# Windowed softmax mix and cosine feed-forward on one core: the prologue's loads, conversions and second softmax in another order

## The chip, the cores and the metric

One core of a Trainium2 chip runs the kernel. The metric is the device time of one execution in microseconds. Three runs of the kernel before gave 2207.27 to 2207.57 us, with a median of 2207.28 us.

The core has a matrix engine (TensorE: PE in the profile, and PEld for its weight loads), a vector engine (VectorE, DVE), an activation engine (ScalarE, ACT), a general engine (GpSimd, POOL) and a sync engine (SyncE, SP) that here issues every transfer. Each engine takes its instructions strictly in the order in which the program lists them, and an instruction waits on semaphores for what it needs from the others.

## The reference

```python
w = np.exp(weight_gen - np.max(weight_gen, axis=-1, keepdims=True))
w = w / (np.sum(w, axis=-1, keepdims=True) + 1e-09)            # 8 heads, 7 taps
x_unf = x_pad[:, idx, :].reshape(B, S, K, H, group)             # a causal window of 7 rows
x = np.einsum('bshk,bskhg->bshg', w, x_unf).reshape(B * S, D)   # 32768 x 192
h = x @ w_in                                                    # 192 x 2048
g = h * np.cos(h)
return (g @ w_out).astype(np.float32)                           # 2048 x 192
```

`x` and `weight_gen` are 32 bits wide; `w_in` and `w_out` arrive as 64-bit words, which the kernel converts itself.

## The kernel before

**Blocks.** Each of the 128 partitions owns 256 consecutive rows of x. A block `b` is four of them in every partition, so there are 64 blocks of 512 rows. For each block the rows are mixed with their taps (`attention`: seven products on line 316 and six adds on line 331, all on POOL), turned over by PE, cut into a high and a low half (`split`: `x_hi` on ACT, `x_b` and `x_lo`), multiplied with `w_in` (`ffn_in_first` and `ffn_in_second`), taken through the cosine by ACT and DVE, cut into halves again (`ghi` on ACT, `glo` on DVE) and multiplied with `w_out` (`ffn_out`). The mixed rows of a block are called `xa` in the trace.

**The loop.** The main loop runs over `i`; eight values of `i` (pairs of 128-column slices of the hidden layer) make a block. In iteration `i` PE does the first product of `i` and the second product of `j = i - 8`. The tile `h` for the hidden values has three buffers in PSUM, and a buffer comes free when DVE has written `glo` (L449). From block 3 on the rows are turned over one at a time, inside `ffn_out` (L379); blocks 1 and 2 are turned over whole, at `i = 5` and `i = 13` (`transpose_all`, L370), and ACT copies the result out of PSUM (L712) before the tile is used for `h`.

**What sets the order.** The program is written by hand and nothing reorders it: the last lines of the function chain every instruction to the one ahead of it on its engine. The mixing of later blocks is a generator `bg` that is advanced two or three steps in each iteration; `until_mixed(b)` forces the rest of a block's steps ahead of the place that needs it. Block 3 is needed at `i = 14`, and its first row is turned over there.

**Weights.** A piece of `w_in` or `w_out` is loaded as 64-bit words into a buffer `raw` and converted by `two_parts` in steps: a size by ACT (L138) into a tile handed out by `make_room`, three integer steps on DVE (L140, L144, L148), a cast to the high half on ACT (L151, for `w_out` also L153 to the tile `wo_b`), and the low half on POOL (L154). The `raw` buffers are shared with `ghi`: twelve of them, handed round in turn, so that a `ghi` waits for the last reader (L154 on POOL) of the piece that had its buffer. Three pieces are loaded and converted ahead of the loop (`w_b0`, `w_a0`, `w_a1`). The others stand in the table `late`: (iteration after which it is loaded, iteration in which it is converted, kind, piece). `w_in_a` fills `wa_hi` and `wa_lo`, `w_in_b` fills `wb_hi` and `wb_lo`, and `w_out_2(q)` fills `wo` and `wo_b` for a pair of slices. I call the eight pieces of `w_out` wo0 to wo7 below.

**Softmax.** `sm0` makes the taps of block 0, `sm1` those of blocks 1 and 2, `sm2` those of blocks 3 to 6. `early=True` means that the exponential is done by ACT; in that case the sum over the taps and its scaling are done by DVE (L265, L268), and otherwise by POOL (`add_taps`, L189 and L192).

**Ahead of the loop.** Three of the four rows of block 0 are mixed by DVE (`mix_first`, L611 and L623) with PE adding up the parts while it turns them over (L603); the fourth row is mixed by POOL. Then come the conversions of `w_b0` and `w_a0`, the casts of block 0 (`x_hi`, `x_b`, `x_lo`) and `sm1`, then the conversion of `w_a1`, the maximum of `sm2`, and the first steps of block 1's mixing.

**SyncE.** The queue of SP holds the transfers and, among them, a marker after each `ffn_in_first` (`traded`), which ties the following instructions to a buffer that changes hands. A transfer that has to wait holds up what stands behind it on that queue.

Of the kernel before, what the change touches and what calls it, by code (L numbers as in the profile page):

```python
# [50 lines left out]
def tile_softmax_conv_then_cos_ffn(  # L51
# [34 lines left out]
    gpool = ctx.enter_context(tc.tile_pool(name="gpool", bufs=12))  # L86
# [37 lines left out]
    def make_room():  # L124
        sizes = ps_m.tile([P, 2, CT], F32, name="acc")
        room[:] = [sizes[:, n, 0:CW].bitcast(I32) for n in range(2)]
# [104 lines left out]
    def softmax(r0, r1, eng, early=True, to=None):  # L231
        n = (r1 - r0) * H
        if r0 == 0:
            t = const.tile([P, n, K], F32, name="taps0")
        else:
            tile_ = work.tile([P, RW * H, K], F32, name="taps")
            t = tile_[:, 0:n, :]
# [26 lines left out]
        if early:  # L264
            nc.vector.tensor_reduce(out=den, in_=t, axis=AX.X, op=ALU.add)  # L265
        else:
            add_taps(t, den)
        (nc.vector if early else nc.gpsimd).tensor_scalar(  # L268
# [287 lines left out]
    def all_of(*steps):  # L556
# [7 lines left out]
        (-1, 2, w_in_a, (1280, 1792)), (-1, 2, w_out_2, (1,)), (-1, 3, w_out_2, (2,)),  # L564
        (-1, 3, w_in_a, (1792, 2048)), (0, 4, w_out_2, (3,)), (0, 4, w_out_2, (4,)),
        (1, 5, w_out_2, (5,)), (1, 6, w_out_2, (6,)), (2, 6, w_out_2, (7,)),
# [17 lines left out]
    load_rows(0)  # L584
    w_b0 = w_in_b(0)
    w_a0 = w_in_a(0, 256)
    sm1 = softmax(R, 3 * R, nc.gpsimd)
# [18 lines left out]
    def mix_first():  # L606
# [9 lines left out]
        for n, ks in enumerate(((K - 1,), (0, 1), (2, 3), (4, 5))):  # L616
# [7 lines left out]
            add_transposed(tr, pr, range(RV), n == 0)  # L624
        return tr

    all_of(sm0)
    all_of(attention(0, nc.gpsimd, RV, R, "pr"))
    tr0 = mix_first()
    add_transposed(tr0, mixed[0], range(RV, R), False)  # L630
    transposed.add(0)
    make_room()
    go_on(w_b0, 1)
    go_on(w_a0, 1)
    x_hi, x_lo, x_b = parts_of(0)
    nc.scalar.copy(out=x_hi, in_=tr0)
    go_on(w_b0, 3)
    all_of(w_b0)
    nc.scalar.copy(out=x_b, in_=x_hi.bitcast(F32))
    go_on(sm1, 2)  # L640
    go_on(w_a0, 3)
    all_of(w_a0)
    nc.vector.tensor_tensor(out=x_lo, in0=tr0, in1=x_hi.bitcast(F32), op=ALU.subtract)
    go_on(sm1, 3)
    all_of(sm1)
# [10 lines left out]
    sm = sm2  # L656
    FIRST = NPAIR + 1
    for i in range(N + LAG + 1):
# [6 lines left out]
        if converts_now:  # L665
            make_room()
# [40 lines left out]
        all_of(*converts.pop(i - 1, ()))  # L707
        now, later = list(splits), []
        splits.clear()
        if whole is not None:  # L710
            t = work.tile([P, 2, CT], F32, name="part", bufs=2)
            nc.scalar.copy(out=t, in_=whole)  # L712
            later.append(split(b + 1, t, slice(0, CT), nc.vector))
        if 0 <= i - 1 < N:
            dve_fraction(i - 1)
            act_cos(i - 1)
# [15 lines left out]
        if i >= NPAIR - 2:  # L732
            next(sm, None)
        for _ in range(3 if i < 12 or i < 64 and i % 4 == 0 else 2):
# [42 lines left out]
```

## Time and profile before

| what | value |
|---|---|
| median of three runs | 2207.28 us |
| the profiled execution, its own time | 2208.1 us |
| its span | 2206.2 us |
| PE busy | 2151.6 us, 98% |
| POOL busy | 2000.7 us, 91% |
| DVE busy | 1907.6 us, 86% |
| ACT busy | 1862.9 us, 84% |
| mean granted PE clock | 0.99 |

The profiled execution takes 2208.1 us, of which the span from its first to its last instruction is 2206.2 us; it lies 0.8 us above the median of the runs. Rows of the timeline give a start, a duration, the engine, the line, and in brackets how long the engine had been idle before and what released it. `x2` in a row stands for two instructions of the same kind.

### The profile page before, as it was taken

What the parts mean: (1) busy time and instruction counts of PE and PEld (TensorE: products, weight loads), DVE (VectorE), ACT (ScalarE), POOL (GpSimd) and SP (SyncE); (2) the same over time, 40 slices, a digit from 0 to 9 for tenths busy, and PEclk for the clock granted to TensorE, in tenths of its full rate; (3) what the DMA queues carried; (4) which work ended last, traced back from release to release, by engine and by line L of the source; (5) the groups of instructions that cost most, each with busy time, mean ns of one, the idle gap of its engine ahead of it and who ended that gap; (6) DMA issues with size and microseconds to landing.
All of it is one profiled execution on the core that took longest, in us unless ns stands there. A gap on an engine that the chain in (4) does not pass through costs nothing.

```text
span 2206.2 us, 62053 instructions
## 1 busy us (share of the span) xinstructions
PE 2151.6 (98%) x26516; PEld 1676.4 (76%) x26516; DVE 1907.6 (86%) x1671; ACT 1862.9 (84%) x2278; POOL 2000.7 (91%) x1687
## 2 busy tenths in 40 slices
PE   4699999999999999999999999999999999999998
PEld 2478777777777777777777777777877777777777
DVE  7888888888888888888888888888888888888886
ACT  4788888888888888888888888888888888888885
POOL 7999999999999999999999999999899999989830
PEclk8799999999999999999999999999999999999999
DMA  7121221221221221221221221211211212211100
GB/s 182 45 48 34 57 48 42 48 48 43 48 57 31 60 48 30 60 48 39 52 48 39 52 56 30 60 46 33 60 41 46 49 41 49 48 40 45 30 16 19
DMA packets 53282, 105.65 MB, mean 48 GB/s; under 512 B 5790, under 2 KB 42134, under 8 KB 53006
## 3 DMA queue, kind: packets, MB, share of 16 engines
q1 hardware_dynamic: 53006, 101.69, 19.3%
q8 instruction: 208, 3.41, 0.7%
q14 instruction: 68, 0.56, 0.1%
HBM read 76.50 MB, written 25.17 MB: 46 GB/s over the span
## 4 chain that ended last, share of the span: by engine, by line
PE 94%; POOL 4%; DVE 1%; issue 1%; DMA 0%; ACT 0%; SPq 0%; POOLq 0%; DVEq 0%; ACTq 0%
PE acc L491 47%; PE h L417 30%; PE h L400 15%; POOL xa L331 1%; PE acc L379 1%; POOL pr L316 1%; PE h L491 0%; POOL wo L154 0%; DMA xt<-in_x_dram 0%; POOL xa L316 0%; POOL wa_lo L154 0%; POOL taps L249 0%; DVE pr L611 0%; POOL taps L281 0%; DVE glo L449 0%
## 5 line engine op out<-in xcount | busy, mean ns | idle before, releaser
L431 DVE TENSOR_TENSOR turn<-h,turn 128x1024 f32<-128x1024 f32 x512 | 627.1, 1225 | 262.8 <-ACT turn L427 258.0
L491 PE MATMUL acc<-wo,ghi 64*128 64x384 f32 x8096 | 808.7, 337 | 0.3 <-ACT ghi L445 0.2
L491 PEld LDWEIGHTS acc<-wo,ghi 64*128 64x128 f32 x8096 | 724.9, 184 | 54.6 <-ACT part L513 16.4
L435 ACT ACTIVATE turn<-turn 128x1024 f32<-128x1024 f32 x512 | 542.4, 1059 | 199.4 <-DVE turn L431 199.3
L331 POOL TENSOR_TENSOR xa<-xa,pr 128x768 f32<-128x768 f32 (+1 forms) x384 | 698.6, 1819 | 0.8
L438 DVE SCALAR_TENSOR_TENSOR h<-h,turn 128x1024 f32<-128x1024 f32 x512 | 631.2, 1233 | 4.6 <-ACT turn L435 4.6
L449 DVE TENSOR_TENSOR glo<-h,ghi 128x1024 bf16<-128x1024 f32 x512 | 622.1, 1215 | 3.8 <-ACT ghi L445 3.8
L427 ACT ACTIVATE turn<-h 128x1024 int32<-128x1024 f32 x512 | 524.6, 1025 | 89.6 <-PE h L417 79.8
L316 POOL TENSOR_TENSOR pr<-xt,taps 128x768 f32<-128x768 f32 (+1 forms) x384 | 589.1, 1534 | 6.3
L445 ACT CAST ghi<-h 128x1024 fp32r<-128x1024 f32 x512 | 516.4, 1009 | 7.5 <-POOL wb_lo L154 5.7
L491 PE MATMUL acc<-wo_b,glo 64*128 64x192 bf16 x8096 | 462.4, 243 | 0.1
L491 PEld LDWEIGHTS <-glo 64*128 64x128 bf16 (+1 forms) x8128 | 317.6, 94 | 85.4 <-issue 67.4
L400 PE MATMUL h<-x_hi,wa_hi 64*128 64x512 f32 x1024 | 300.3, 581 | 0.0
L417 PE MATMUL h<-x_hi,wa_hi 64*128 64x512 f32 x1024 | 300.1, 581 | 0.0
L400 PE MATMUL h<-x_lo,wa_hi 64*128 64x512 bf16 x1024 | 199.2, 384 | 28.6 <-DVE glo L449 20.8
L417 PE MATMUL h<-x_hi,wb_hi 64*128 64x512 f32 x1024 | 204.6, 395 | 0.0
L400 PE MATMUL h<-x_b,wa_lo 64*128 64x512 bf16 x1024 | 196.6, 379 | 2.3 <-POOL wa_lo L154 2.3
L417 PE MATMUL h<-x_lo,wa_hi 64*128 64x512 bf16 x1024 | 195.7, 378 | 2.5 <-SPq L342 1.8
L417 PE MATMUL h<-x_b,wb_lo 64*128 64x512 bf16 x1024 | 195.9, 378 | 0.0
L417 PE MATMUL h<-x_lo,wb_hi 64*128 64x512 bf16 x1024 | 195.9, 378 | 0.0
L417 PE MATMUL h<-x_b,wa_lo 64*128 64x512 bf16 x1024 | 195.9, 378 | 0.0
L359 POOL TENSOR_SCALAR x_b<-x_hi 128x256 bf16<-128x256 f32 (+1 forms) x246 | 102.9, 418 | 93.0 <-ACT x_hi L357 91.7
(90 smaller groups left out, 1973.1 us busy)
## 6 DMA issues: line engine op xcount, KB each, us to landing
xt<-in_x_dram SPq DMA_DIRECT2D x62, 960.0 KB, 7.0
out_dram<-part SPq DMA_DIRECT2D x256, 96.0 KB, 2.2
taps<-in_weight_gen_dram SPq DMA_DIRECT2D x15, 448.0 KB, 4.4
raw<-in_moe_w_out_dram SPq DMA_DIRECT2D x8, 384.0 KB, 9.4
raw<-in_moe_w_in_dram SPq DMA_DIRECT2D x10, 256.0 KB, 11.5
xt<-in_x_dram SPq DMA_DIRECT2D x1, 768.0 KB, 11.5
xt<-in_x_dram SPq DMA_DIRECT2D x1, 540.0 KB, 5.5
raw<-in_moe_w_in_dram SPq DMA_DIRECT2D x4, 128.0 KB, 7.9
```

The lines of the kernel that those rows point to most:

```text
L316: eng.tensor_tensor(out=dst.rearrange("p r (h g) -> p r h g", h=H), in0=xt[:, k + ra:k + rb, :].rearrange("p r (h g) -> p r h g", h=H), in ...
L331: eng.tensor_tensor(out=acc if k < K else xa, in0=acc, in1=old[:, ra:rb], op=ALU.add)
L359: nc.gpsimd.tensor_scalar(out=near[:, :, cs], in0=hi[:, :, cs].bitcast(F32), scalar1=1.0, scalar2=1.0, op0=ALU.mult, op1=ALU.mult)
L400: nc.tensor.matmul(h[:, q, :], lhsT=w[rs, chunk(pair, q)], rhs=v[rs, q, :], start=(m == 0), stop=False, skip_group_check=True)
L417: nc.tensor.matmul(h[:, 1 - q, :], lhsT=w[rs, cs], rhs=v[rs, q ^ middle, :], start=False, stop=(m == len(prods) - 1), skip_group_check=True)
L427: nc.scalar.activation(out=t.bitcast(I32), in_=hs[i], func=AF.Identity, bias=0.25, scale=1.0)
L431: nc.vector.tensor_tensor(out=t, in0=hs[i], in1=t.bitcast(I32), op=ALU.subtract)
L435: nc.scalar.activation(out=t, in_=t, func=AF.Sin, bias=SIN_BIAS, scale=SIN_SCALE)
L438: nc.vector.scalar_tensor_tensor(out=hs[i], in0=hs[i], scalar=TWO_PI, in1=turns.pop(i), op0=ALU.mult, op1=ALU.mult)
L445: nc.scalar.copy(out=hi, in_=hs[i])
L449: nc.vector.tensor_tensor(out=lo, in0=hs.pop(i), in1=hi.bitcast(F32), op=ALU.subtract)
L491: nc.tensor.matmul(to, lhsT=g[rs, n, t * P:(t + 1) * P], rhs=w[rs, fc, :], start=(lo == 0 and c == 0 and (k == 0 or whole and k == 1)), st ...
```

## The change

Nothing that is computed changes. The order of the prologue does, in seven places:

1. The taps of block 0 are taken in rising order (0, then 1 and 2, 3 and 4, 5 and 6); before, tap 6 came first.
2. The two pieces `w_a0` and `w_b0` trade places, in their loads and their conversions.
3. `sm1` is moved forward: its maximum stands among the products of `mix_first`, and its steps among the conversions of `w_a0` and `w_b0`. Its sum over the taps is done by POOL (`on_dve=False`).
4. The buffers shared by `raw` and `ghi` become thirteen.
5. In the table `late`, four pieces are loaded after iteration 0 instead of ahead of the loop, and the pieces of `w_out` from wo3 on are converted one an iteration (wo3 at 4, wo4 at 5, up to wo7 at 8) where before wo3 and wo4 stood at 4 and wo6 and wo7 at 6. The size of the piece at iteration 8 goes to an SBUF tile (`part`), since by then the PSUM tile `acc` is in use.
6. In the iteration in which a block is turned over whole, ACT's copy of it (`part<-h`) stands ahead of the casts of the weights converted then; before it stood behind them.
7. The generator `bg` is advanced by two steps instead of three for `i` below 8; `sm2` takes its last steps one iteration later.

```diff
-    gpool = ctx.enter_context(tc.tile_pool(name="gpool", bufs=12))
+    gpool = ctx.enter_context(tc.tile_pool(name="gpool", bufs=13))
...
-    def make_room():
-        sizes = ps_m.tile([P, 2, CT], F32, name="acc")
+    def make_room(home="acc"):
+        sizes = ps_m.tile([P, 2, CT], F32, name="acc") if home == "acc" else (
+            work.tile([P, 2, CT], F32, name="part", bufs=2))
...
-    def softmax(r0, r1, eng, early=True, to=None):
+    def softmax(r0, r1, eng, early=True, to=None, on_dve=None):
...
-        if early:
+        if on_dve:
             nc.vector.tensor_reduce(out=den, in_=t, axis=AX.X, op=ALU.add)
...
-        (-1, 3, w_in_a, (1792, 2048)), (0, 4, w_out_2, (3,)), (0, 4, w_out_2, (4,)),
-        (1, 5, w_out_2, (5,)), (1, 6, w_out_2, (6,)), (2, 6, w_out_2, (7,)),
+        (0, 3, w_in_a, (1792, 2048)), (1, 4, w_out_2, (3,)), (1, 5, w_out_2, (4,)),
+        (1, 6, w_out_2, (5,)), (1, 7, w_out_2, (6,)), (2, 8, w_out_2, (7,)),
...
+    w_a0 = w_in_a(0, 256)
     w_b0 = w_in_b(0)
-    w_a0 = w_in_a(0, 256)
-    sm1 = softmax(R, 3 * R, nc.gpsimd)
+    sm1 = softmax(R, 3 * R, nc.gpsimd, on_dve=False)
...
-        for n, ks in enumerate(((K - 1,), (0, 1), (2, 3), (4, 5))):
+        for n, ks in enumerate(((0,), (1, 2), (3, 4), (5, 6))):
...
+            if n == 2:
+                go_on(sm1, 3)
...
+    make_room()
+    go_on(w_a0, 1)
+    go_on(w_b0, 1)
     tr0 = mix_first()
...
-    make_room()
-    go_on(w_b0, 1)
-    go_on(w_a0, 1)
+    go_on(sm1, 1)
+    go_on(w_a0, 3)
+    all_of(w_a0)
     x_hi, x_lo, x_b = parts_of(0)
     nc.scalar.copy(out=x_hi, in_=tr0)
-    go_on(w_b0, 3)
+    go_on(w_b0, 2)
+    go_on(sm1, 1)
+    go_on(w_b0, 1)
+    nc.scalar.copy(out=x_b, in_=x_hi.bitcast(F32))
+    all_of(sm1)
     all_of(w_b0)
-    nc.scalar.copy(out=x_b, in_=x_hi.bitcast(F32))
-    go_on(sm1, 2)
-    go_on(w_a0, 3)
-    all_of(w_a0)
     nc.vector.tensor_tensor(out=x_lo, in0=tr0, in1=x_hi.bitcast(F32), op=ALU.subtract)
-    go_on(sm1, 3)
-    all_of(sm1)
...
-            make_room()
+            make_room("acc" if j < 0 else "part")
...
-        all_of(*converts.pop(i - 1, ()))
         now, later = list(splits), []
         splits.clear()
         if whole is not None:
             t = work.tile([P, 2, CT], F32, name="part", bufs=2)
             nc.scalar.copy(out=t, in_=whole)
             later.append(split(b + 1, t, slice(0, CT), nc.vector))
+        all_of(*converts.pop(i - 1, ()))
...
-        if i >= NPAIR - 2:
+        if NPAIR - 1 <= i <= NPAIR + 1:
+            next(sm2, None)
+        if i >= FIRST:
             next(sm, None)
-        for _ in range(3 if i < 12 or i < 64 and i % 4 == 0 else 2):
+        for _ in range(3 if NPAIR <= i < 12 or 12 <= i < 64 and i % 4 == 0 else 2):
```

The lines of the changed kernel lie one to four below those of the kernel before (L316 is L318 there, L331 is L333, L154 is L155, L151 is L152, L712 is L716). The first place is the list of POOL between the mixing of block 0 and the first product of block 1 (`xa<-xt,taps 128x768`). Before:

```order
L154 TENSOR_TENSOR wb_lo<-raw,wb_hi 128x512
L249 TENSOR_TENSOR taps<-taps,top 128x448
L154 TENSOR_TENSOR wa_lo<-raw,wa_hi 128x256
L281 TENSOR_TENSOR taps<-taps,den 128x448
L249 TENSOR_TENSOR taps<-taps,top 128x896
L154 TENSOR_TENSOR wa_lo<-raw,wa_hi 128x512
L316 TENSOR_TENSOR xa<-xt,taps 128x768
```

In the changed kernel (128x448 are the taps of `sm1`, 128x896 those of `sm2`):

```order
L251 TENSOR_TENSOR taps<-taps,top 128x448
L190 TENSOR_TENSOR side<-taps 128x64x3
L193 TENSOR_TENSOR den<-side 128x64
L193 TENSOR_TENSOR den<-den,side 128x64
L193 TENSOR_TENSOR den<-den,taps 128x64
L270 TENSOR_SCALAR den<-den 128x64
L155 TENSOR_TENSOR wa_lo<-raw,wa_hi 128x256
L283 TENSOR_TENSOR taps<-taps,den 128x448
L155 TENSOR_TENSOR wb_lo<-raw,wb_hi 128x512
L251 TENSOR_TENSOR taps<-taps,top 128x896
L155 TENSOR_TENSOR wa_lo<-raw,wa_hi 128x512
L318 TENSOR_TENSOR xa<-xt,taps 128x768
```

The subtraction of `sm1` moved from behind `wb_lo` to the head of the list, and five small instructions for its sum came in.

The second place is POOL's list around the end of block 1's mixing and the start of block 2's. Before:

```order
L316 TENSOR_TENSOR pr<-xt,taps 128x768
L331 TENSOR_TENSOR xa<-xa,pr 128x768 x2
L154 TENSOR_TENSOR wa_lo<-raw,wa_hi 128x512
L154 TENSOR_TENSOR wo<-raw,wo 128x2x192
L316 TENSOR_TENSOR xa<-xt,taps 128x768
L316 TENSOR_TENSOR pr<-xt,taps 128x768
L154 TENSOR_TENSOR wo<-raw,wo 128x2x192
L154 TENSOR_TENSOR wa_lo<-raw,wa_hi 128x256
L316 TENSOR_TENSOR pr<-xt,taps 128x768
```

In the changed kernel:

```order
L333 TENSOR_TENSOR xa<-xa,pr 128x768
L155 TENSOR_TENSOR wo<-raw,wo 128x2x192
L155 TENSOR_TENSOR wa_lo<-raw,wa_hi 128x256
L333 TENSOR_TENSOR xa<-xa,pr 128x768
L155 TENSOR_TENSOR wo<-raw,wo 128x2x192
L318 TENSOR_TENSOR xa<-xt,taps 128x768
L318 TENSOR_TENSOR pr<-xt,taps 128x768
L155 TENSOR_TENSOR wo<-raw,wo 128x2x192
L361 TENSOR_SCALAR x_b<-x_hi 128x1024
```

The last add of block 1 is now followed at once by the low half of wo3, and after two products of block 2 by that of wo4 and by `x_b` of block 1; before, the pieces there were a slice of `w_in`, wo1 and wo2, and wo3 came four products and an add later.

The third place is ACT's list in iteration 5, with `part<-h` for the copy of block 1 and `turn<-turn` for a cosine. Before:

```order
L427 ACTIVATE turn<-h 128x1024
L445 CAST ghi<-h 128x1024
L151 CAST wo<-raw 128x2x192
L153 CAST wo_b<-raw 128x384
L151 CAST wo<-raw 128x2x192
L153 CAST wo_b<-raw 128x384
L712 COPY part<-h 128x1024
L435 ACTIVATE turn<-turn 128x1024
```

In the changed kernel, up to the cast of wo4 in the next iteration:

```order
L447 CAST ghi<-h 128x1024
L716 COPY part<-h 128x1024
L152 CAST wo<-raw 128x2x192
L154 CAST wo_b<-raw 128x384
L437 ACTIVATE turn<-turn 128x1024
L139 ACTIVATE acc<-raw 128x384
L429 ACTIVATE turn<-h 128x1024
L447 CAST ghi<-h 128x1024
L152 CAST wo<-raw 128x2x192
```

The copy of block 1 moved ahead of the cast of wo3, and the cast of wo4 moved behind the next iteration's `turn<-h`.

More of the change, by code (lines that the diff above doesn't have):

```diff
@@ L229, in powers @@
         yield
-    def softmax(r0, r1, eng, early=True, to=None):
+    def softmax(r0, r1, eng, early=True, to=None, on_dve=None):
         n = (r1 - r0) * H
+        on_dve = early if on_dve is None else on_dve
         if r0 == 0:
@@ L267, in softmax @@
             add_taps(t, den)
-        (nc.vector if early else nc.gpsimd).tensor_scalar(
+        (nc.vector if on_dve else nc.gpsimd).tensor_scalar(
             out=den, in0=den, scalar1=1e-9 / (1.0 if early else EXP_UNIT), scalar2=TWO_PI,
@@ L563, in tile_softmax_conv_then_cos_ffn @@
         (-1, 0, w_in_a, (768, 1280)), (-1, 1, w_in_b, (1,)), (-1, 1, w_out_2, (0,)),
-        (-1, 2, w_in_a, (1280, 1792)), (-1, 2, w_out_2, (1,)), (-1, 3, w_out_2, (2,)),
-        (-1, 3, w_in_a, (1792, 2048)), (0, 4, w_out_2, (3,)), (0, 4, w_out_2, (4,)),
-        (1, 5, w_out_2, (5,)), (1, 6, w_out_2, (6,)), (2, 6, w_out_2, (7,)),
+        (0, 2, w_in_a, (1280, 1792)), (0, 2, w_out_2, (1,)), (0, 3, w_out_2, (2,)),
+        (0, 3, w_in_a, (1792, 2048)), (1, 4, w_out_2, (3,)), (1, 5, w_out_2, (4,)),
+        (1, 6, w_out_2, (5,)), (1, 7, w_out_2, (6,)), (2, 8, w_out_2, (7,)),
     ]
@@ L654, in tile_softmax_conv_then_cos_ffn @@
     N = NB * NPAIR
-    sm = sm2
+    sm = None
     FIRST = NPAIR + 1
```

## The prediction

> **What bounds the kernel now.** I read the page first, then the waits of PE behind the prologue, then the timeline of each engine in the first 120 us, since the change touches nothing later: the lists of all engines hold the same instructions in the same order again from about iteration 21 on.
>
> ```profile
> span 2206.2 us, 62053 instructions
> PE acc L379 <- POOL xa L331: 0.9, 1, 0.9
> PE acc L491 <- ACT ghi L445: 0.2, 1, 0.2
> 111.36 3.75 POOL L331 TENSOR_TENSOR xa<-xa,pr 128x768 f32<-128x768 f32 x2
> 115.16 0.28 PE L379 MATMUL acc<-ident,xa 64*128 64x64 f32 x2 [0.85 <-POOL xa L331]
> 30.09:115.06 84.97, 83.78 (x57) 0.78 0.29 75
> ```
>
> Rows two and three are all the waits of PE from 110 us to 2190 us, 1.1 us. So behind 115.16 PE runs flat, and whatever the prologue does reaches the end only as a shift of that moment. What PE waited for there is row four: POOL ends the mixing of block 3 at 115.1, and PE turns its first row over. Row six is POOL's busy time from its first product of block 1 (30.09) to that end: 83.78 of 84.97 us, and the rest is gaps of hundredths between instructions. POOL has no slack in this stretch. The end of the prologue is therefore the start of block 1 on POOL, plus 85 us of work, plus every microsecond that POOL stands still in between. In the changed kernel the same 57 instructions lie between these two marks, in another order. This is the sum I make.
>
> **The start on POOL: sooner by 3.7 us.**
>
> ```profile
> 7.16 0.52 POOL L316 TENSOR_TENSOR xa<-xt,taps 128x192 f32<-128x192 f32 x1 [4.45 <-DMA xt<-in_x_dram]
> 9.06 0.75 DVE L611 TENSOR_TENSOR pr<-xt,h 128x576 f32<-128x576 f32 x1 [3.06 <-DMA xt<-in_x_dram]
> 5.82 1.24 SPq L238 DMA_DIRECT2D taps<-in_weight_gen_dram  x2
> taps<-in_weight_gen_dram SPq DMA_DIRECT2D x1, 224.0 KB, 7.4
> 16.24 0.76 DVE L623 TENSOR_TENSOR pr<-h,pr 128x576 f32<-128x576 f32 x1
> 18.97 0.61 DVE L246 TENSOR_REDUCE top<-taps 128x64 f32<-128x448 f32 x1
> 20.76 1.22 DVE L643 TENSOR_TENSOR x_lo<-h,x_hi 128x1024 bf16<-128x1024 f32 x1
> 22.03 0.96 POOL L249 TENSOR_TENSOR taps<-taps,top 128x448 f32<-128x448 f32 x1
> 24.99 1.03 DVE L246 TENSOR_REDUCE top<-taps 128x128 f32<-128x896 f32 x1
> 26.15 1.75 POOL L249 TENSOR_TENSOR taps<-taps,top 128x896 f32<-128x896 f32 x1
> 28.11 0.65 ACT L151 CAST wa_hi<-raw 128x512 fp32r<-128x512 f32 x1 [3.99 <-DVE raw L148]
> 28.84 1.29 POOL L154 TENSOR_TENSOR wa_lo<-raw,wa_hi 128x512 bf16<-128x512 f32 x1 [0.94 <-ACT wa_hi L151]
> 30.09 1.55 POOL L316 TENSOR_TENSOR xa<-xt,taps 128x768 f32<-128x768 f32 x1
> L189 POOL TENSOR_TENSOR side<-taps 128x384 f32<-128x384 f32 x14 | 13.0, 930 | 0.0
> L192 POOL TENSOR_TENSOR den<-den,taps 128x128 f32<-128x128 f32 x14 | 7.6, 543 | 1.1
> 26.54 0.61 PE L417 MATMUL h<-x_lo,wa_hi 64*128 64x512 bf16 x2 [1.76 <-SPq L342]
> 49.15 1.01 ACT L445 CAST ghi<-h 128x1024 fp32r<-128x1024 f32 x1 [5.74 <-POOL wb_lo L154]
> ```
>
> Tap 6 needs rows of the second transfer of x, which DVE awaits until 9.06; tap 0 needs only the first, which POOL already uses at 7.16. DVE's mixing starts 1.9 us sooner, but the maximum of `sm1` (0.61 us) now stands ahead of the last pair of taps and waits for its transfer (5.82 + 7.4 = 13.2). The last add moves from 16.24 to about 15.45, and with the order of the two conversions turned round `x_lo` moves from 20.76 to about 20.2: 0.6 us.
>
> The larger part is behind it. Before, `sm1` began on POOL only at 22.03, and DVE took up the maximum of `sm2` only at 24.99, behind the sum of `sm1`. Now the exponential and the sum of `sm1` run while DVE still mixes and converts: POOL's five added instructions take about 1.9 us for 64 columns (0.93 and 0.54 us for 128 columns, in the two groups of rows above, taken in proportion), on an otherwise idle POOL. So DVE goes from `x_lo` (ends 21.4) to the maximum (1.0), then the three integer steps of `w_a1` (0.72 each, ending 24.4); ACT casts until 25.07, POOL's `wa_lo` takes 1.3, and block 1 starts at 26.4 in place of 30.09: **-3.7 us**. A later transfer or cast could leave 2.8 of it, an earlier `x_lo` give 4.6.
>
> The edits to the loads have one answer: SP no longer holds PE's marker behind four waiting transfers in iteration 0 (1.76 us of PE at 26.54, off POOL's path), and the last pieces land by about 45 us, ahead of their use. The thirteenth buffer removes the wait of ACT for `wb_lo` ahead of 49.15; that makes ACT, DVE and PE earlier by up to 11 us until block 2, and POOL not at all.
>
> **The chain that the new order closes: 7.2 us.** Up to the last add of block 1, POOL has seven products, six adds, three pieces of 512 columns, three of `w_out` and one of 256: 28.7 us from its start to start times, so it is there at 55.1. Following ACT and DVE with the same durations, the casts that it needs on the way are all done 2 us or more ahead. There the next instruction is the low half of wo3, which needs ACT's cast; ACT now has the copy of block 1 ahead of that cast; the copy needs PE's eight turnings; and these need the add that POOL has just finished. POOL stands still for the whole round.
>
> ```profile
> 63.10 0.54 ACT L151 CAST wo<-raw 128x384 fp32r<-128x384 f32 x1 [1.33 <-DVE raw L148]
> 59.14 1.94 PE L370 MATMUL h<-ident,xa 128*128 128x128 f32 x8 [3.37 <-DVE glo L449]
> 64.86 1.00 ACT L712 COPY part<-h 128x1024 f32<-128x1024 f32 x1
> 65.92 0.61 PE L400 MATMUL h<-x_lo,wa_hi 64*128 64x512 bf16 x2 [4.84 <-ACT part L712]
> 70.24 1.03 ACT L427 ACTIVATE turn<-h 128x1024 int32<-128x1024 f32 x1 [3.00 <-PE h L417]
> 72.06 0.57 ACT L151 CAST wo<-raw 128x384 fp32r<-128x384 f32 x1
> 73.92 1.04 ACT L357 CAST x_hi<-part 128x1024 fp32r<-128x1024 f32 x1
> 106.61 1.10 PE L370 MATMUL h<-ident,xa 128*128 128x128 f32 x8
> 67.02 1.99 POOL L154 TENSOR_TENSOR wo<-raw,wo 128x384 fp32r<-128x384 f32 x2
> ```
>
> Before, wo3 was converted at 67.02, long after its cast at 63.10. Now: turnings 1.94 (PE has idled for some 5 us by then, and turned at that rate after 3.4 us of idling; 1.10 where it was running), copy 1.00, cast 0.55, three handovers: wo3 starts 3.55 us after the add, at 58.65. **+3.55**, at least 2.7.
>
> wo3 and two products take POOL to 62.6. wo4 needs a cast that stands behind iteration 6's `turn<-h`, which awaits PE's products of iteration 5, and these await the copy. From the copy's end (58.15) the rows give 65.92 to 70.24, 4.3 us, to `turn<-h`, and 1.8 us and 0.55 more to the end of the cast: 64.9. **+2.3**; with PE at the faster rate of the turnings (1.10 to 1.94, so 2.4 us for the products) 0.4. Then `x_b` of block 1, after wo4 at 65.9, needs `x_hi`, which ends 2.9 us behind the start of wo4's cast (72.06 to 73.92, plus 1.04), at 67.25: **+1.35** at either rate.
>
> **Later terms.**
>
> ```profile
> 79.37 1.22 DVE L362 TENSOR_TENSOR x_lo<-part,x_hi 128x1024 bf16<-128x1024 f32 x1
> 79.56 2.42 POOL L316 TENSOR_TENSOR pr<-xt,taps 128x768 f32<-128x768 f32 x1
> 116.86 2.33 DVE L362 TENSOR_TENSOR x_lo<-part,x_hi 128x1024 bf16<-128x1024 f32 x1
> 118.07 2.02 POOL L359 TENSOR_SCALAR x_b<-x_hi 128x1024 bf16<-128x1024 f32 x1
> 84.39 0.61 PE L400 MATMUL h<-x_lo,wa_hi 64*128 64x512 bf16 x2 [8.25 <-DVE glo L449]
> 90.15 1.57 PE L491 MATMUL acc<-wo,ghi 64*128 64x384 f32 x16
> 94.25 0.39 PE L400 MATMUL h<-x_lo,wa_hi 64*128 64x512 bf16 x2
> 98.33 1.57 PE L491 MATMUL acc<-wo,ghi 64*128 64x384 f32 x16
> ```
>
> wo5 and wo6 are in time within 0.6 us. wo7 now comes after iteration 8's DVE work; following DVE and ACT, its cast ends at about 83, some 0.7 us after POOL is ready for it. Its two bitwise steps on DVE now read both inputs from SBUF. The first two rows above show what that costs: while DVE's `x_lo` read two SBUF tiles, POOL's product took 2.42 us instead of 1.55, and the next pair has DVE at 2.33 for 1.22 until POOL's instruction ended. I take **+1.2** for wo7, between 0 and 1.8. The Trainium skill (SBUF — State Buffer, Who interferes with whom) says that a VectorE instruction with two SBUF inputs and a GpSimd instruction that reads SBUF exclude each other for the whole instruction; the four rows agree, and by that page alone the term would be at its upper end.
>
> The same pair of `x_lo` and POOL for block 2 fell behind 115.1 before (the 116.86 row). Now PE, ACT and DVE reach iteration 14 some 10 us sooner than POOL, so it falls into the stretch: **+1.0**, at least 0.
>
> Last, PE reaches the turning of block 3 at about 106 and waits there for POOL until about 121. Before, after 8.25 us of idling, it took 90.15 - 84.39 = 5.76 us from a first product to the next output product, where 98.33 - 94.25 = 4.08 is the running value. That restart, **+1.7** (0 if it kept its rate, 1.9 at most by half rate over 4 us), now lies on the path; before it lay at 84.39, where POOL was the later one anyway.
>
> Sum: -3.7 + 3.55 + 2.3 + 1.35 + 1.2 + 1.0 + 1.7 = +7.4 us. On the profiled execution that is a span of 2213.6 and a time of 2215.5 us; on the median, which lay 0.8 us below it, 2214.7 us. With every term at its low end: -4.6 + 2.7 + 0.4 + 1.35 = -0.15; at its high end: -2.8 + 3.55 + 2.3 + 1.35 + 1.8 + 1.1 + 1.9 = +9.2.
>
> How soon PE regains its rate decides the second wait. Here all the products from 65.92 to 70.24 ran slow; the Trainium skill (TensorE: Matmul & The Clock Gate, What's actually happening) gives about 3.4 us of sustained work, and by an estimate from that page 0.9 us of the products would run at double rate, the wait would shrink by 0.45, and the sum be +6.95.
>
> **Rivals.**
>
> *PE runs at its rate through iteration 5, and the two engines don't collide.* Then 2.7 + 0.4 + 1.35 of waits, wo7 0.7, restart 1.7, start -3.7: +3.15, 2210.4 us. For it: only 1.1 us of idling lies between the turnings and the products. Against: the 4.3 us of slow products followed turnings in the trace too. 0.17.
>
> *POOL doesn't wait.* If POOL got to wo3 when its cast is long done, only the early start would count: -3.7, with the restart at the turning of block 3 still added (PE waits some 5 us there) -2.0, 2205.3 us. That needs ACT's copy to be done before POOL's last add of block 1, which the order excludes unless that add ends later than I have it against its neighbours. 0.12.
>
> *PE, not POOL, sets the end.* PE starts iteration 8 at 73 instead of 84.4, because nothing holds up `ghi` any more and the copy of block 1 comes 6.7 us sooner; it loses 2.5 us in iteration 10 to late `glo`, and is 8.9 us ahead: 2198.4 us, faster by 0.4%. It decides if POOL ends block 3 by 106.2, which would leave it 79.8 us after its start for 85 us of work. The window's 83.78 busy microseconds speak against it, unless POOL's instructions run shorter beside other neighbours, or the start comes sooner than the transfers let me see. 0.06.
>
> *The early start doesn't come*: the maximum of `sm1` or the raw words of `w_a1` land later than in the trace of before, and the waits are added to a start at 30: up to +11, 2218.3 us. 0.07.
>
> **The numbers.** The forecast holds 0.58. A difference of 0.2% is 4.4 us, which is about what a measurement of this kernel can tell from none. The forecast's own range is 2210 to 2217; a tenth of it lies within 0.2%. Faster: 0.07, from the third rival and a little of the second. Same: the first rival, most of the second and that tenth, 0.34. Slower: 0.59, the rest of the forecast and the fourth rival. The range goes from 2205, which takes in the second rival, to 2217, and leaves out the third and the fourth.
>
> **What would show it.** In the changed profile: POOL's first product of block 1 at 26 to 27 us; POOL idle ahead of wo3 for 3 to 4 us with ACT's cast as releaser, again ahead of wo4 and `x_b`; PE's first row of block 3 at 120 to 122 with more than 8 us of idling before it, released by POOL, at a low clock after it. I am wrong if POOL shows under 4 us of idling between 27 and 120 us, or if that row of PE lies ahead of 115.

## The result and the profile after

The changed kernel takes 2220.31 us (median of 6 runs, 2219.68 to 2221.21), the kernel before, beside it on the same chip, 2207.51 us (6 runs, 2207.27 to 2208.9). The ratio is 1.0058 with a 95% interval of 1.0045 to 1.0071: slower by 12.8 us. The forecast was 2214.7 and the range ended at 2217. The direction was right, the size too small by 5.6 us. The profiled execution took 2220.37 us.

The span on the page of the changed kernel, and all its waits of PE from 110 to 2190 us (engine, tile, line, releaser: total us, times, longest):

```profile
span 2218.6 us, 62049 instructions
```

```profile
PE acc L381 <- POOL xa L333: 13.7, 1, 13.7
PE h L402 <- POOL x_lo L364: 1.8, 1, 1.8
```

Before, these waits were 1.1 us in all. So nearly all of the difference still passes through one point, the first row of block 3 on PE, and there is a second, later wait that was not there. PE's timeline at that point, with the first two rows of block 3 and the first product behind the second wait:

```profile
123.99 0.37 PE L381 MATMUL acc<-ident,xa 64*128 64x64 f32 x2 [13.71 <-POOL xa L333]
...
130.03 0.22 PE L381 MATMUL acc<-ident,xa 64*128 64x64 f32 x2
...
201.49 0.39 PE L402 MATMUL h<-x_lo,wa_hi 64*128 64x512 bf16 x2 [1.79 <-POOL x_lo L364]
```

The first row comes at 123.99 instead of 115.16: +8.83. From there to the second row PE takes 6.04 us; before it was 115.16 to 118.67, 3.51 us: +2.53. Behind the second row the span has 2088.57 us left, before 2087.53: +1.04. The three add up to the 12.4 us between the spans (2206.2 and 2218.6). I split the span of every kernel below into these three numbers.

POOL's timeline between its start on block 1 and that row; only the rows with more than 1 us of idling are shown, and around the first of them the instruction ahead.

```profile
26.18 1.54 POOL L318 TENSOR_TENSOR xa<-xt,taps 128x768 f32<-128x768 f32 x1
...
53.08 1.80 POOL L333 TENSOR_TENSOR xa<-xa,pr 128x768 f32<-128x768 f32 x1
58.47 1.02 POOL L155 TENSOR_TENSOR wo<-raw,wo 128x384 fp32r<-128x384 f32 x1 [3.58 <-ACT wo L152]
...
64.28 1.02 POOL L155 TENSOR_TENSOR wo<-raw,wo 128x384 fp32r<-128x384 f32 x1 [1.79 <-ACT wo L152]
66.62 1.04 POOL L361 TENSOR_SCALAR x_b<-x_hi 128x1024 bf16<-128x1024 f32 x1 [1.32 <-ACT x_hi L359]
...
84.56 1.02 POOL L155 TENSOR_TENSOR wo<-raw,wo 128x384 fp32r<-128x384 f32 x1 [2.52 <-ACT wo L152]
...
98.97 1.01 POOL L524 TENSOR_TENSOR part<-part 128x384 f32<-128x384 f32 x1 [3.06 <-ACT part L515]
```

Block 1 starts 3.91 us sooner, and five waits take 12.27 us. Four of them were forecast; the last was not. Its chain, in the order in which one releases the next:

```profile
89.19 1.54 POOL L318 TENSOR_TENSOR pr<-xt,taps 128x768 f32<-128x768 f32 x1
...
90.76 0.54 SPq L240 DMA_DIRECT2D taps<-in_weight_gen_dram  x1
...
95.37 0.62 DVE L248 TENSOR_REDUCE top<-taps 128x64 f32<-128x448 f32 x1 [4.04 <-DMA taps<-in_weight_gen_dram]
...
97.15 1.06 ACT L437 ACTIVATE turn<-turn 128x1024 f32<-128x1024 f32 x1 [2.23 <-DVE turn L433]
98.12 0.78 ACT L515 COPY part<-acc 128x768 f32<-128x768 f32 x1
```

POOL's last product of block 2 ends at 90.7 and frees the buffer of its taps (there are two). Only then can SP send the taps of blocks 7 to 10. In the profile SP's queue had waited 5.8 us for that product. DVE, which takes the maximum of these taps at the end of iteration 10, stands still for 4.04 us until they land. ACT's cosine and its copy `part` come late, and POOL, which began all this, waits for the copy. Before, the same transfer and the same maximum stood like this:

```profile
93.25 0.54 SPq L238 DMA_DIRECT2D taps<-in_weight_gen_dram  x1
...
99.05 0.61 DVE L246 TENSOR_REDUCE top<-taps 128x64 f32<-128x448 f32 x1
```

SP issued it later than in the changed kernel, and DVE still didn't wait: it took up that maximum only at 99.05, since PE, ACT and DVE were nearly 8 us further behind (99.05 against 91.3, where DVE now began to wait).

### The profile page after: what moved, and what is told of

The parts are those of the page before. It is cut to its first block, busy times and chain, and to the rows that moved or that the text cites. A ratio compares the mean times of both kernels' runs of the same rounds, so it can differ in the third digit from the quotient of the medians.

```text
span 2218.6 us, 62049 instructions
## 1 busy us (share of the span) xinstructions
PE 2154.4 (97%) x26516; PEld 1681.8 (76%) x26516; DVE 1907.3 (86%) x1669; ACT 1861.4 (84%) x2278; POOL 2000.7 (90%) x1692
## 3 DMA queue, kind: packets, MB, share of 16 engines
q8 instruction: 208, 3.41, 0.7%
## 4 chain that ended last, share of the span: by engine, by line
PE 91%; POOL 5%; DVE 1%; DMA 1%; issue 1%; ACT 1%; SPq 0%; POOLq 0%; ACTq 0%; DVEq 0%
PE acc L493 46%; PE h L419 29%; PE h L402 15%; POOL xa L333 2%; POOL pr L318 2%; PE acc L381 1%; DMA taps<-in_weight_gen_dram 1%; DMA raw<-in_moe_w_out_dram 0%; PE h L493 0%; POOL x_lo L364 0%; DVE turn L433 0%; DVE glo L451 0%; ACT turn L437 0%; POOL wo L155 0%; POOL xa L318 0%
## 5 line engine op out<-in xcount | busy, mean ns | idle before, releaser
L333 POOL TENSOR_TENSOR xa<-xa,pr 128x768 f32<-128x768 f32 (+1 forms) x384 | 698.8, 1820 | 0.7
L318 POOL TENSOR_TENSOR pr<-xt,taps 128x768 f32<-128x768 f32 (+1 forms) x384 | 588.3, 1532 | 6.1
```

Source lines behind the costliest of these rows:

```text
L318: eng.tensor_tensor(out=dst.rearrange("p r (h g) -> p r h g", h=H), in0=xt[:, k + ra:k + rb, :].rearrange("p r (h g) -> p r h g", h=H), in ...
L333: eng.tensor_tensor(out=acc if k < K else xa, in0=acc, in1=old[:, ra:rb], op=ALU.add)
```

## The experiments

"First row" is the first row of block 3 on PE, "to second" the time from it to the second row, "behind" what is left of the span behind the second. Times are medians; the other three numbers come from the one profiled execution of each kernel, which lay up to 1.0 us from its median. In these executions POOL began block 1 between 25.3 and 26.2 us in all kernels with the early start, so a difference of less than 1 us in the first row says nothing. The kernel before had 2207.1 to 2207.5 us beside each group.

| kernel | us | first row | to second | behind |
|---|---|---|---|---|
| before | 2207.3 | 115.16 | 3.51 | 2087.53 |
| changed | 2220.31 | 123.99 | 6.04 | 2088.57 |
| 1 ACT's copy behind the casts | 2220.27 | 123.01 | 5.48 | 2088.91 |
| 2 all later softmaxes one iteration later | 2232.72 | 119.91 | 5.20 | 2106.59 |
| 3 three steps of `bg` | 2208.29 | 111.52 | 6.23 | 2088.45 |
| 4 before, with the start alone | 2203.06 | 111.45 | 3.51 | 2087.14 |
| 5 only the first softmax later | 2217.01 | 120.39 | 5.28 | 2089.13 |
| 6 run 4 and the thirteenth buffer | 2203.65 | 110.84 | 3.52 | 2087.54 |
| 7 PE kept busy | 2218.43 | 123.44 | 3.50 | 2089.16 |
| 8 pieces of w_out as before | 2217.85 | 120.69 | 6.29 | 2088.72 |
| 9 without edit 7 | 2203.80 | 111.20 | 3.52 | 2086.98 |
| 10 run 9 and PE kept busy | 2206.51 | 115.13 | 3.46 | 2086.61 |
| 11 run 6 and two steps | 2221.68 | 125.56 | 5.50 | 2088.84 |
| 12 only the softmax's half of edit 7 undone | 2221.18 | 124.38 | 5.99 | 2088.43 |

**Run 1: is it the place of ACT's copy?** Edit 6 undone: `all_of(*converts.pop(i - 1, ()))` again ahead of the copy.

> The changed kernel with ACT's copy of a block that is turned over whole put back behind the casts of that iteration. Theory (a ring through POOL, PE and ACT): wo3's low half no longer waits, since its cast is done by 54, but wo4's cast still stands behind the products of iteration 5, which stand behind PE's turnings, which stand behind POOL's last add of block 1; so wo4 still starts at 64.3, the 3.6 us of idling ahead of wo3 moves to wo4 (1.8 to about 5.4), block 3 ends at 123.9 as before the edit, and the time stays at 2220.3 within 1 us. Rival (the place of the copy is itself the cost): POOL gets the 3.6 us back, 2216.7.

The time stayed (ratio to before 1.006, 1.0043 to 1.0077). POOL's waits in this kernel, from 26 to 125 us:

```profile
POOL wo L155 <- ACT wo L152: 8.0, 2, 5.9
POOL part L524 <- ACT part L515: 2.6, 1, 2.6
POOL x_b L361 <- ACT x_hi L359: 1.3, 1, 1.3
```

The wait ahead of wo3 went and the one ahead of wo4 grew to 5.9, as expected: the same round of POOL, PE, ACT and back, only at the next piece. Where the copy stands decides which piece pays for it.

**Run 2: the late taps.** All softmaxes of the loop begin one iteration later.

```diff
-    FIRST = NPAIR + 1
+    FIRST = NPAIR + 2
```

> The changed kernel with the softmax of blocks 7 to 10 begun one iteration later (10 instead of 9). Theory (the transfer of its taps waits for a buffer that POOL still reads until 90.7, lands at 95.4, and DVE's maximum in iteration 10 holds up the cosine behind it): DVE's wait of 4.0 us shrinks to under 1, PE no longer waits 1.8 us for SP, POOL's wait ahead of its add on part (3.1) goes to under 0.5, and the time falls by 2.7 to 3 us, to 2217.4. Rival (POOL waits there because PE's products of iteration 11 are late anyway): no change, 2220.3.

A miss. The first row did come sooner, at 119.91, with no wait of DVE or POOL for the taps. But all fifteen softmaxes moved against the rest of their blocks, and PE now waits in nearly every one of them, as its waits behind 107 us show:

```profile
PE h L402 <- POOL x_lo L364: 21.4, 14, 2.7
```

The edit changed two things, so it proves nothing of the time. Run 5 is the clean form.

**Run 3: the pace of the mixing.** Three steps of `bg` for i below 8; the softmax stays as in the changed kernel.

```diff
-        for _ in range(3 if NPAIR <= i < 12 or 12 <= i < 64 and i % 4 == 0 else 2):
+        for _ in range(3 if i < 12 or i < 64 and i % 4 == 0 else 2):
```

> The changed kernel with three steps of the mixing in each iteration below 8, as before the change; nothing else. Theory (POOL meets wo3 with nothing else to do): now six instructions of block 2 stand between block 1's last add and wo3, so the waits ahead of wo3, wo4 and x_b are all gone (6.7 us), and block 2's last product comes early enough to free the taps' buffer (3.1 us); a wait of up to 3 us stays ahead of wo7. Block 3 ends at 112 to 114, PE idles some 4 us ahead of it: 2205.5 to 2208. Rival (the conversions one an iteration, with the casts behind PE's products, are the cost whatever POOL does between): POOL still idles over 5 us, 2215 or more.

12.0 us of the loss are gone (ratio 1.0005, 0.9995 to 1.0014); the time lies 0.3 us above what was expected. POOL waits for no cast of w_out, and ends block 3 at 111.5. PE still idles ahead of that row and restarts slowly, and POOL waits behind it:

```profile
111.52 0.37 PE L381 MATMUL acc<-ident,xa 64*128 64x64 f32 x2 [4.35 <-POOL xa L333]
...
117.75 0.21 PE L381 MATMUL acc<-ident,xa 64*128 64x64 f32 x2
...
120.49 1.01 POOL L524 TENSOR_TENSOR part<-part 128x384 f32<-128x384 f32 x1 [4.03 <-ACT part L515]
```

**Run 4: the start alone.** The kernel before with edits 1 to 3 and nothing else.

> The kernel before with only the first three edits: rising taps, w_a0 ahead of w_b0, and the second softmax moved forward with its sum on POOL. Buffers, table, copy and step counts as before. Theory (POOL is busy throughout, so its start is what counts): block 1 starts on POOL at 26.2 instead of 30.1, no new wait comes in, block 3 ends at 111.2, and the time falls by 3.9 us to 2203.6. Rival (the transfers, or PE's marker behind them on SP, hold the early start back later on): POOL idles by as much as it gained, 2207.5.

It beats both kernels: ratio to before 0.9982 (0.9972 to 0.9991), 4.1 us by the medians of all runs. The 3.7 us of the forecast's first term are there (111.45 for 115.16), and nothing takes them back.

**Run 5: the late taps, cleanly.** Only the first softmax of the loop begins one iteration later.

```diff
-        if i % (SB * NPAIR) == FIRST and b + 6 < NB:
+        if i % (SB * NPAIR) == FIRST and b + 6 < NB and i > FIRST or i == FIRST + 1:
...
-        if i >= FIRST:
+        if i > FIRST:
```

> The changed kernel, with the first softmax of the loop alone (taps of blocks 7 to 10) begun one iteration later, at i = 10; all later ones keep their place. If the freed buffer of the taps is what holds POOL ahead of the last steps of block 2 (3.1 us at 98.97 in the changed kernel: POOL awaits ACT's part, behind DVE's maximum of taps that land at 95.4), that wait goes, PE's first row of block 3 comes at about 120 us instead of 123.99, and the time falls by 3 to 4 us, to 2216.3 to 2217.4. Rival: the stretch behind block 3 is set by something else, PE's own later waits for POOL take the gain, and the time stays at 2219.5 to 2220.5.

3.3 us sooner than the changed kernel, and the first row 3.6 us sooner (0.46 of it from an earlier start on POOL in this execution), both as expected. DVE finds the taps landed, and POOL goes from product to `part` without a gap:

```profile
94.08 1.55 POOL L318 TENSOR_TENSOR xa<-xt,taps 128x768 f32<-128x768 f32 x1
...
95.59 1.02 POOL L524 TENSOR_TENSOR part<-part 128x384 f32<-128x384 f32 x1
95.61 0.61 DVE L248 TENSOR_REDUCE top<-taps 128x64 f32<-128x448 f32 x1
```

The missed term of some 3 us is this one.

**Run 6: the thirteenth buffer.** Run 4 with `bufs=13`.

> The version with the changed start alone (edits 1 to 3), and now the thirteenth buffer besides. POOL's order and waits are the same, so the first row of block 3 stays at 111.4 us. Theory: the thirteenth buffer lets PE, ACT and DVE run some 9 us ahead of POOL, so PE idles 5 to 10 us ahead of that row, restarts slowly (2.4 us in the changed kernel) and meets a later wait of up to 1.8 us: 2205.5 to 2207.3, 2.4 to 4.2 us slower than the 2203.1 of the version without it. Rival: idling of PE costs nothing by itself, the time stays at 2202.7 to 2203.8. Second rival: the wait of ghi for its buffer shifts POOL's neighbours and the row itself moves.

The theory fell: 2203.65 us, within 0.6 us of run 4. ACT's wait for `wb_lo` is gone, but the early start had already cut it from 5.7 us to 1.4 in run 4, and PE gets no lead from the rest; it stands as long as before ahead of iteration 8, for `glo`:

```profile
80.16 0.61 PE L401 MATMUL h<-x_lo,wa_hi 64*128 64x512 bf16 x2 [8.79 <-DVE glo L450]
```

The idling ahead of the row of block 3, on which theory and rival differed, didn't arise, so this run doesn't show what such idling costs.

**Run 7: PE's slow restart.** The changed kernel, with PE computing the first product of iteration 14 nineteen times over (the same values).

```diff
-        for m, (w, v) in enumerate(((wa_b, x_lo), (wa_lo, x_b), (wa_hi, x_hi))):
+        again = 19 if i == 14 else 1
+        for m, (w, v) in list(enumerate(((wa_b, x_lo), (wa_lo, x_b), (wa_hi, x_hi)))) * again:
```

> The changed kernel, with PE computing the first product of iteration 14 nineteen times over instead of once (the same values again, so that it works through most of the 13.7 us in which it waits for POOL). POOL is untouched, so the first row of block 3 stays at about 124 us. Theory: the slow restart of PE is the lowered rate after idling, so with PE busy the 2.1 to 2.4 us from that row to the first product of iteration 16 are won back, and up to 1.8 us more where POOL and DVE had to catch up at i = 32: 2216.4 to 2218.2. Rival: the loss is the refilling of the chain of engines, not PE's rate: 2219.5 to 2220.7.

1.9 us by the medians, 0.2 us less than the least that was expected, and far from the rival. The windows view gives the granted clock (in each row the third number from the right); the first two rows are the changed kernel behind the first row of block 3, the third is this one.

```profile
124.00:130.00 6.00, 6.00 (x46) 4.78 (x48) 0.70 (x1) 1.76 (x2) 3.95 (x3) 0.55 0.12 33
130.00:136.00 6.00, 6.00 (x86) 4.51 (x83) 4.86 (x5) 4.89 (x6) 3.07 (x3) 1.00 0.01 3
```

```profile
123.40:126.90 3.50, 3.46 (x46) 3.00 (x48) 0.10 (x1) 1.16 (x2) 3.50 (x3) 1.00 0.20 54
```

The same 46 matmuls take 6.0 us at a granted clock of 0.55 and 3.5 us at 1.00. So the restart between these two rows is the clock. The later wait of PE for `x_lo` stays (2.4 us in two pieces), so it doesn't come from the restart.

**Run 8: the pieces of w_out.** The changed kernel with wo3 to wo7 at iterations 4, 4, 5, 6, 6 as before.

> The changed kernel with the conversions of wo3 to wo7 back at iterations 4, 4, 5, 6 and 6 (loads as in the changed kernel). Theory: the wait ahead of wo3 stays at 3.5 to 3.6 us, since it comes from the copy of the whole block; those ahead of wo4 (1.8) and wo7 (2.5) go, the one ahead of x_b (1.3) stays or moves to wo5, and the wait for the late taps shrinks to 1 to 3 us; the first row of block 3 at 118 to 120 us, time 2214.5 to 2216.5. Rival: one piece an iteration is the whole cost, the ring of copies doesn't hold POOL without it: 2207.5 to 2209. Second rival: the pieces' places don't matter: 2219.5 to 2220.5.

The first row is sooner by 3.3 us and the time by 2.5, where 4 to 6 were expected. wo7's wait is all but gone (0.27 us ahead of wo6 and wo7 together) and wo3's stays, as the theory had it; but wo4's 1.79 us moved to wo5 as 1.29, and the wait for the taps hardly shrank (2.87). Both rivals are out.

```profile
58.14 2.00 POOL L155 TENSOR_TENSOR wo<-raw,wo 128x384 fp32r<-128x384 f32 x2 [3.58 <-ACT wo L152]
...
64.42 1.02 POOL L155 TENSOR_TENSOR wo<-raw,wo 128x384 fp32r<-128x384 f32 x1 [1.29 <-ACT wo L152]
...
95.67 1.01 POOL L524 TENSOR_TENSOR part<-part 128x384 f32<-128x384 f32 x1 [2.87 <-ACT part L515]
```

One piece an iteration costs what wo7 waits; the other waits stand without it.

**Run 9: without edit 7.** Pace and softmax as before.

```diff
-    sm = None
+    sm = sm2
...
-        if NPAIR - 1 <= i <= NPAIR + 1:
-            next(sm2, None)
-        if i >= FIRST:
+        if i >= NPAIR - 2:
             next(sm, None)
-        for _ in range(3 if NPAIR <= i < 12 or 12 <= i < 64 and i % 4 == 0 else 2):
+        for _ in range(3 if i < 12 or i < 64 and i % 4 == 0 else 2):
```

> The changed kernel without the whole of edit 7: three steps of the mixing for i below 8, and the last steps of the softmax of blocks 3 to 6 one iteration sooner, as before. Theory: POOL waits for no cast of w_out and ends block 3 at 111.0 to 111.6 us, as with three steps alone; PE comes 3 to 5 us sooner, idles and restarts slowly (6.0 us from the first to the second row of block 3, where 3.5 is the running value); but POOL now has more of block 4 in hand, so that it doesn't idle for 4 us ahead of part, and PE's later wait of 1.8 us for x_lo at i = 32 is gone: 2206.5 to 2207.4, about 1 to 1.8 us under the 2208.29 of three steps alone. Rival: that later wait comes from the slow restart itself, and the time stays at 2207.8 to 2208.8.

Better than either theory: 2203.80 us (ratio to before 0.9985, 0.9976 to 0.9994), 16.5 us under the changed kernel. The later wait and POOL's 4 us ahead of `part` are gone, as expected. The slow restart at block 3 is gone too, because PE does its idling elsewhere. Two rows of PE:

```profile
90.15 0.88 PE L493 MATMUL acc<-wo,ghi 64*128 64x384 f32 x4 [4.04 <-POOL wo L155]
...
111.20 0.27 PE L381 MATMUL acc<-ident,xa 64*128 64x64 f32 x2 [0.97 <-POOL xa L333]
```

PE waits 4.04 us at 90.15, for the low half of wo7, at a place where POOL is the later one anyway, and only 0.97 us at the row.

**Run 10.** Run 9, with PE repeating the first product of iteration 14 seven times (`again = 7`).

> The kernel without edit 7, and PE computes the first product of iteration 14 seven times over (the same values again), 4.0 us more work in the time in which it waits for POOL. Theory: the second row of block 3 comes 3.5 instead of 6.0 us behind the first, the first at 111.0 to 111.6, and the time is 2.5 us below that of the same kernel without the repeats: 2203.8 to 2205.0. Rival: what PE wins there it loses again to POOL, as when PE repeated the product nineteen times (1.9 us of 2.5 were left): 2205.0 to 2206.0.

The time lies above both ranges, which rested on an idle stretch that run 9 turned out not to have. The 4.0 us of repeats had no gap to fill; PE sets the row itself (115.13), and the time rises by 2.7 us. It tells nothing of the restart.

**Run 11: the pace alone.** Run 6 with the two steps of the changed kernel and no other part of edits 5 to 7.

> The version with the changed start and the thirteenth buffer (2203.65 us), and of the rest only the slower pace: two steps of the mixing instead of three for i below 8. The casts of wo3 and wo4 stand ahead of the copy of block 1 here, so the wait falls on wo5. Theory: the slower pace alone closes the ring: POOL waits 4 to 5 us ahead of wo5, 1.3 ahead of x_b and 1 to 3 for the late taps, ends block 3 at 118 to 120 us, PE idles and restarts slowly: 2214 to 2217. Rival: without one piece an iteration and the copy moved forward, POOL gets to the pieces when their casts are done: 2203 to 2205.

The pace alone makes the whole loss and more: 18 us over run 6. Its price I had too low. POOL waits at more places than in the changed kernel; the longest:

```profile
59.47 1.99 POOL L154 TENSOR_TENSOR wo<-raw,wo 128x384 fp32r<-128x384 f32 x2 [3.17 <-ACT wo L151]
...
68.00 1.01 POOL L154 TENSOR_TENSOR wo<-raw,wo 128x384 fp32r<-128x384 f32 x1 [3.54 <-ACT wo L151]
...
100.54 1.02 POOL L523 TENSOR_TENSOR part<-part 128x384 f32<-128x384 f32 x1 [3.00 <-ACT part L514]
```

The copy of block 1 stands behind the casts of wo3 and wo4 here, and the ring shows ahead of wo5, with 3.54 us. The 3.17 us ahead of wo3 are not the ring: ACT's cast at 58.85 waited there for DVE's last step on that piece. POOL with too little to do between the pieces meets late casts of either kind.

**Run 12: the softmax's place alone.** Run 9's diff without its last two lines.

> The changed kernel with only the second half of edit 7 undone: the last steps of the softmax of blocks 3 to 6 one iteration sooner, the pace still two steps for i below 8. On POOL only its last instruction of that softmax (1.75 us) moves, from behind wo7 to three instructions ahead of it. Theory: the slower pace is the cause and the softmax's place only adds where the mixing of block 3 has come up to it, so this undoes little: the 1.75 us now fill most of the 2.5 us in which POOL waits for the cast of wo7, the waits ahead of wo3, wo4, x_b and for the late taps stay (3.6, 1.8, 1.3, 3.1), the first row of block 3 comes at 121.9 to 122.8 us, the slow restart and PE's later wait stay: 2218.2 to 2219.3. Rival: each half of edit 7 has its own price, 12 us for the pace and 4.5 for the softmax's place, as the steps from 2220.3 over 2208.3 to 2203.8 read: 2215 to 2216.5.

No gain: 2221.18 us, above both ranges. The 1.75 us did cover wo7 in part (1.07 us of waiting for 2.52), but wo6 now waits 1.71, which the theory had missed. Each half's own price, the rival, is refuted: with the slow pace the softmax's place is worth nothing, with the fast one 4.5 us (runs 3 and 9).

## Why the prediction was right in direction and wrong in size

The main mechanism was the right one: POOL without slack, stopped ahead of wo3, wo4 and `x_b` by a round over PE and ACT that outweighs the early start. Of the signs that the prediction named all came but one: PE's first row of block 3 was to come at 120 to 122 us and came at 123.99. Point by point, forecast and then measured:

| term | forecast | measured |
|---|---|---|
| start of block 1 on POOL | -3.7 | -3.91 |
| wait ahead of wo3 | +3.55 | +3.58 |
| wait ahead of wo4 | +2.3 | +1.79 |
| wait ahead of `x_b` | +1.35 | +1.32 |
| wo7 | +1.2 | +2.52 |
| POOL beside `x_lo` of block 2, and other durations (what is left of the 8.83) | +1.0 | +0.47 |
| wait for the late taps | none | +3.06 |
| PE's restart | +1.7 | +2.53 |
| later, behind the second row | none | +1.04 |
| sum | +7.4 | +12.4 |

**The step that failed** is the list of later terms: it followed DVE and ACT through iterations 8 to 10 with their engines' durations, and asked of no transfer but those of the weights whether it would still be there when PE and DVE came sooner. So it put at nothing a wait that took 3.06 us. The prediction gave the edits to the loads "one answer", off POOL's path; the taps of blocks 7 to 10 aren't among those loads, but their buffer is freed by POOL, which was late, and read by DVE, which was early. In the trace of before that transfer showed no wait, and by an estimate had only some 1.2 us of slack: issued at 93.25, it would have landed at 97.9 with the 4.6 us that it took from 90.76 to 95.37 in the changed kernel, and DVE took it up at 99.05. Run 5 removes the term and 3.3 us with it. The same wait held PE up: it was to reach the row of block 3 at 106 us, reached it at 110.3 (123.99 less 13.71 of idling), and in run 5 at 106.8.

The next largest errors are sizes, wo7 and the restart, and the 1.04 us behind the second row, for which the forecast had no term and whose cause stays open.

**wo7** had the right place and too small a size. The piece waits for ACT, and ACT for PE's products of iteration 8:

```profile
72.57 0.61 PE L402 MATMUL h<-x_lo,wa_hi 64*128 64x512 bf16 x2 [4.81 <-DVE glo L451]
...
75.51 2.93 PE L493 MATMUL acc<-wo,ghi 64*128 64x384 f32 x16 [1.49 <-DVE raw L149]
...
82.13 1.03 ACT L429 ACTIVATE turn<-h 128x1024 int32<-128x1024 f32 x1 [2.23 <-issue]
```

PE idled ahead of iteration 8, then waited 1.49 us more, because the PSUM tile `acc` still held the size of wo6, and ran its output products at half rate (2.93 us for 16, where 1.57 was the running value). For ACT's row at 82.13 the profile names no releaser, but PE's last product of iteration 8 ends at 82.03. I had counted the cast's own steps and not these. Run 8, with wo7 back at iteration 6, has 0.27 us of waiting ahead of wo6 and wo7 together.

**The restart** was sized from one row of before (1.7 us) and bounded by 1.9. In the eight kernels with a long wait it was 1.7 to 2.8 us. Run 7 shows that it is the granted clock; the last section shows what sets its length.

**wo4** was oversized since PE regained its rate within iteration 5: its products took from 58.01 to 61.8 instead of the 4.3 us of before. That is the variant that the prediction gave by the Trainium skill (TensorE: Matmul & The Clock Gate, What's actually happening), a wait smaller by 0.45 us; it came out smaller by 0.51. That the two agree so closely is partly luck: the estimate counts 3.4 us of work from the first product, and the full clock came back at 61.1, which is 3.1 us behind that product, at a moment that the product doesn't set (see the last section).

**The collision** came as forecast, DVE at 2.69 us for 1.22 and POOL at 2.40 for 1.55; with the other durations of POOL +0.47 us are left of it:

```profile
112.83 2.69 DVE L364 TENSOR_TENSOR x_lo<-part,x_hi 128x1024 bf16<-128x1024 f32 x1
...
114.51 2.40 POOL L318 TENSOR_TENSOR pr<-xt,taps 128x768 f32<-128x768 f32 x1
```

**Which edit does it** the prediction had only in part. It put the closed ring down to the copy that stands ahead of the cast (edit 6); run 1 shows that this place changes nothing. Edit 7 closes it. What counts is how much work POOL's list holds between the last add of block 1, for which PE waits, and the first piece whose cast stands behind that round (wo3 in the changed kernel, wo4 in run 1, wo5 in run 11). In the kernel before, from the end of that add (55.2) to wo3 (67.02), POOL had nine instructions to do, of which these are the first and the last:

```profile
55.22 1.30 POOL L154 TENSOR_TENSOR wa_lo<-raw,wa_hi 128x512 bf16<-128x512 f32 x1
...
65.52 1.55 POOL L316 TENSOR_TENSOR pr<-xt,taps 128x768 f32<-128x768 f32 x1
```

That is 11.8 us of cover for a round that takes 3.6 us to wo3 and 9.4 us to wo4 (54.9 to 64.28 in the changed kernel). Two steps an iteration instead of three leave nothing between the two instructions. With three steps, and the softmax's place as before, the late pieces, the copy's place and one piece an iteration together cost nothing (run 9 beside run 6: 2203.80 and 2203.65); with two steps no other part of edits 5 to 7 is needed for the loss (run 11). Two steps without the early start were not tried.

**What stays open.** The later wait of PE for `x_lo` at i = 32, about 1 us on the end, is there in the kernels in which POOL reaches `part` 2.7 to 5.1 us too early behind block 3 (changed, 1, 3, 5, 7, 8, 11 and 12, and run 2 among its other waits; 2.3 us in run 10 brought none), whether PE restarted slowly or not (run 7), and is gone in run 9, where POOL has two more instructions of block 4 to do first. How the one leads to the other over sixteen iterations was not followed. Runs 4, 6 and 9, all faster than before, lie within 0.8 us of each other, and I don't rank them.

## What to carry to other kernels

When an engine without slack hands work to another and later needs its answer, read in its list how much of its own work lies between the two instructions, and compare it with the round trip; an edit that only slows a background generator can take that cover away without touching either instruction. When a change makes engines earlier at one place and another engine later, go through every transfer and buffer between them, also those that never waited in the trace. Try the parts of a bundle apart: here the first three edits were worth 4 us, and the last one, a few lines on the pace of a generator, cost more than 16.

## What the runs showed of the hardware

The slow stretch of PE after idling has no fixed length, and the idling doesn't set it. By the granted clock, which was 0.50 in it and 1.00 behind it, it lasted from the first row of block 3 for 5.4 us after 13.71 us of idling (changed), 5.8 after 4.35 (run 3), 3.7 after 13.59 (run 5) and 6.0 after 13.72 (run 8); 3.5 was the shortest of the eight kernels with a long wait (run 2). After 1.54 us of idling (run 7) there was none.

What sets it is where the row falls among marks that lie 3.41 us apart, and whose place in the span differs from execution to execution. The clock changes only at such marks: it is 0.50 from 112.30 to 129.36 us in the changed kernel, which is five times 3.41, and from 110.49 to 117.32 in run 3, which is twice. In all eight kernels the full clock came back at the second mark behind the row, so that the slow stretch lay between one and two steps of 3.41 us. The Trainium skill (TensorE: Matmul & The Clock Gate, What's actually happening) has the full rate return after at least one busy window of about 3.4 us, in a window that runs free of the kernel. The marks agree with that. Where the page says that only the first 3.4 us or so run slowly, and that the moment varies by 0.5 us either way, the 3.5 to 6.0 us measured here decide.

An integer step of DVE took nearly three times as long when its tile lay in SBUF and POOL was at work. The size of wo6 is in PSUM (`acc`), that of wo7 in SBUF (`part`), with the same shape:

```profile
73.64 0.56 DVE L141 TENSOR_SCALAR acc<-acc 128x384 int32<-128x384 int32 x1
...
80.63 1.63 DVE L141 TENSOR_SCALAR part<-part 128x384 int32<-128x384 int32 x1
```

The second has one SBUF input. It began 0.13 us behind a product of POOL (80.50 and 1.55 us long) and ended 0.2 us behind its end. In runs 1, 2, 5 and 7 it took 1.63 to 1.65 us at the same place; in run 9, where it began as an instruction of POOL ended, 0.38. The prediction had expected such a block at the two steps behind it, which read two SBUF tiles. These ran in 0.56 us, since POOL was by then waiting; in run 9, where POOL was at work, they took 2.08 and 1.99. ACT's cast of wo7 didn't wait for any of this: at 83.94 it came right behind the cast `ghi` (83.05).
